# Experts' gate sums: PSUM banks copied by ScalarE and their diagonal picked by transfers, in place of a masked sum on VectorE

## The chip, the cores and the metric

The kernel runs on one NeuronCore of a Trainium2 chip. The metric is the device time of one execution in microseconds; a time is a median over runs. The engines are TensorE (matmuls), VectorE (DVE in the profile), ScalarE (ACT), GpSimd (POOL) and SyncE (SP, here a queue that issues transfers). ScalarE and SP also issue transfers (ACTq and SPq in the profile). Each engine works through its own instructions in the order in which the program wrote them, and a wait holds up everything behind it on that engine.

## The reference

The kernel mixes two branches with a gate. The input x has 2048 tokens of 640 values.

```python
g = sigmoid((x * gate_w).sum(-1, keepdims=True))
a = einsum("ts,se->te", seq_re, x @ hid_re.T) - einsum("ts,se->te", seq_im, x @ hid_im.T)
s1, s2 = scores of 32 heads against two sets of 16 keys (q = x @ w_q, split in two)
top 2 of s1, top 2 of s2 -> 4 sums -> top 2 pairs (e1, e2) -> softmax of the two
b[n] = sum over heads and the two pairs of gate * gelu(x[n] @ u[e]) * v[e],  e = 16 * e1 + e2
out = g * a + (1 - g) * b
```

The kernel doesn't gather rows of u and v. It computes gelu(x u) for all 256 experts, and for each token a table of 256 numbers: the sum of the gates of all (head, pair) choices that fell on expert e. The table multiplies the activations, and a matmul with v gives b. The change concerns only how this table gets from the matmuls that make it into DRAM.

## The kernel before, in words

**The stages.** The Fourier branch is done first along the sequence: two matrices (real, imaginary; `w`), four columns of 512 tokens each (`c`), 16 pieces of 128 source tokens each (`s`), so 128 pieces (`seq_piece`, L200). A piece is 128 x 512 f32 values, loaded by SP five pieces ahead (L158) and split three pieces ahead into a high and a low part: ScalarE writes the high part (L122), GpSimd subtracts (L123). Four buffers `WS` hold split pieces. Five groups of three matmuls (`mm3`, L127 to L129) add the piece into PSUM banks 0 to 4. After 16 pieces ScalarE evicts the five banks to `ST` (L217), VectorE multiplies them by the gate row (`gate_piece`, L191), and ScalarE's queue stores them to `pd` in DRAM (L198). In between the pieces the scores (L409 to L421), the activations (`u_pair`, L528) and the choice of experts (`topk`, `gates`, `rows`) are worked off. The last part, from piece 128 on, multiplies by the hidden matrices in two halves `b` of 35 steps (`step`, L846), with loads of `pd` and sums of them on VectorE (`add_a`, L738), and adds the experts' part (`z_group`, L832).

**The pump.** What VectorE has to do beside the main row is written as generators that yield an estimate of their time. `run_bg` is called after each group of three matmuls with 0.68 (us of TensorE), and adds `share` times this to a credit; as long as the credit is positive the next step is written into the program. The share is 1.25 while the experts run, 0.95 from eight pieces before the last part (`ending`, L935), 0 in the first ten steps of the last part and 1.05 after. Gate pieces, table sums (`make_sums`, L673) and the like take their estimate from the credit. `bg.drain` writes all steps left until a condition holds: at four pieces before the last part, until two of the sets are free (L946), and in `load_z`, until the half's sums are complete (L763).

**The experts.** `experts` (L555) works through 32 sets: two halves `g` of 1024 tokens, 16 chunks `c` of 64 tokens (eight of each of the half's eight 128-token tiles). `build` writes two one-hot f16 tables for a set with three VectorE instructions (L570 to L572): P[r, (e1, t)], which carries the gate, and Q[r, (e2, t)]; rows r are the (part of the gate, choice, head) combinations, 128 of them, and t counts four tokens that are handled together. `use` (L587) multiplies them: 16 matmuls of 128 x 64 by 64 (L594) fill one PSUM bank of 128 partitions x 8 x 64. A partition is (half s, e1, t) and a column (m, e2, t'); only t = t' is wanted, the rest are products of different tokens. Sets are handed out in pairs, singly once `ending` is set. The matmuls of a pair are written after the next pair's tables. Banks 5 and 6 are used in turn (`ps_s`), bank 7 in the last part.

**The sums.** `sums` (L574) takes the diagonal t = t' on VectorE. A mask `mask4` of 128 x 4, with 1/32768 where t' is the partition's t and 0 elsewhere, multiplies the bank (L578, into `tmp`), and a reduction over t' (L580) writes 16 x 8 values per partition into `cd`, a buffer of 128 x 16 x 128. The step is charged 1.4. After the sixteenth chunk of a half SP writes `cd` to `gd` in DRAM with two transfers (L584), one for each 64 partitions. `load_z` (L760) later reads `gd` back, 128 expert rows x 128 tokens at a time (L770), together with the activations and the gate row, on SP's queue.

Of the kernel before, what the change touches and what calls it, by code (L numbers as in the profile page):

```python
# [8 lines left out]
F32 = mybir.dt.float32  # L9
F32R = mybir.dt.float32r  # L10
F16 = mybir.dt.float16
AF = mybir.ActivationFunctionType
OP = mybir.AluOpType
AX = mybir.AxisListType
PSUM = bass.MemoryType.PSUM

P = 128
# [3 lines left out]
E = 16  # L21
# [12 lines left out]
GSCALE = 32768.0  # L34
# [56 lines left out]
def gated_mix_kernel(ctx: ExitStack, tc: tile.TileContext, xT, xn, dreT, dimT, wsre, wsim, wq, kT, uT, vv, gw, out):  # L91
    nc = tc.nc
    ctx.enter_context(tc.manual_schedule())

    const = ctx.enter_context(tc.tile_pool(name="const", bufs=1))
    big = ctx.enter_context(tc.tile_pool(name="big", bufs=1))
    dram = ctx.enter_context(tc.tile_pool(name="dram", bufs=1, space=bass.MemoryType.DRAM))
# [8 lines left out]
    def bank(n, shape=(P, TC), dt=F32):  # L106
        return psum.tile(list(shape), dt, name=f"b{n}", tag=f"b{n}")

    def ps_s(shape=(P, TC)):
        return bank(5 + rotate("pss", 2), shape)  # L110

    def ps_t(shape, dt=F32):
        return bank(7, shape, dt)
# [16 lines left out]

    pd = {(w, c): dram.tile([KD, P, TC], F32, name=f"pd{w}{c}", tag=f"pd{w}{c}") for w in range(2) for c in range(NC)}
    actd = dram.tile([2, P, S], F32, name="actd")
    gd = dram.tile([2, 2, 4, E, E, P], F32, name="gd")
    gdr = dram.tile([S], F32, name="gdr")
    bg = Pump()

# [42 lines left out]
    p3, last_part, ending, share = None, False, False, 0.95  # L179
# [40 lines left out]
    for q in range(2 * NC):  # L220
        n = NT * (q + 1)
# [50 lines left out]
    t = ps_t([P, 512])  # L272
# [12 lines left out]
    for r in range(2):  # L285
# [3 lines left out]
    identf = const.tile([P, P], F32)  # L289
# [3 lines left out]
    wtab4 = const.tile([P, E, 4], F16)  # L293
    nc.gpsimd.iota(wtab4, pattern=[[-1, E], [0, 4]], base=E, channel_multiplier=0,
                   allow_small_or_imprecise_dtypes=True)
    mask4 = const.tile([P, 4], F32)
    nc.vector.tensor_reduce(mask4, identf.rearrange("p (a b) -> p b a", b=4), op=OP.add, axis=AX.X)
    nc.vector.tensor_scalar(mask4, mask4, 1.0 / GSCALE, None, op0=OP.mult)


    wqs, wps, wp = {}, {}, {}
# [68 lines left out]
    n = bursts[-1]  # L370
# [170 lines left out]
    for p in range(NP):  # L541
        n = N0 + 5 * p
# [12 lines left out]
    def experts():  # L555


        shp = [P, 16, E, 4]
        wt = wtab4[:, None].to_broadcast(shp)
        todo = deque((g, c) for g in range(2) for c in range(16))  # L560
        cd = {}

        def build(g, c, s):
            pt, qt = (HOT[s // 2][:, s % 2, n].rearrange("p (m e t) -> p m e t", e=E, t=4) for n in range(2))

            def row(n):
                r = ROWS[g][:, n, 8 * c:8 * c + 8, :].rearrange("p b (s t) -> p (b s) t", t=4)
                return r[:, :, None, :].to_broadcast(shp)

            nc.vector.tensor_tensor(pt, row(0), wt, op=OP.is_equal)  # L570
            nc.vector.tensor_tensor(qt, row(1), wt, op=OP.is_equal)
            nc.vector.tensor_tensor(pt, pt, row(2), op=OP.mult)  # L572

        def sums(g, c, t):  # L574
            if c == 0:
                cd[g] = p3.tile([P, E, P], F32, name="cd", tag="cd")
            tmp = p3.tile([P, 8 * E, 4], F32, name="tmp")
            nc.vector.tensor_tensor(tmp, t.rearrange("p m (e t) -> p (m e) t", t=4),  # L578
                                    mask4[:, None, :].to_broadcast([P, 8 * E, 4]), op=OP.mult)
            nc.vector.tensor_reduce(cd[g][:, :, 8 * c:8 * c + 8].rearrange("p e m -> p m e"),  # L580
                                    tmp.rearrange("p (m e) t -> p m e t", e=E), op=OP.add, axis=AX.X)
            if c == 15:
                for s in range(2):
                    nc.sync.dma_start(gd[g, s].rearrange("t e f m -> e t f m"), cd[g][64 * s:64 * s + 64])  # L584
                summed.add(g)

        def use(group):  # L587
            ts = []
            for g, c, s in group:
                t = bank(7, (P, 8, E * 4)) if last_part else ps_s((P, 8, E * 4))  # L590
                pt, qt = (HOT[s // 2][:, s % 2, n].rearrange("p (m c) -> p m c", m=16) for n in range(2))
                for m in range(16):
                    r = slice(64 * (m % 2), 64 * (m % 2) + 64)
                    nc.tensor.matmul(t[r, m // 2, :], pt[:, m], qt[:, m], start=True, stop=True)  # L594
                ts.append(t)
                free_sets.append(s)
            for (g, c, s), t in zip(group, ts):
                sums(g, c, t)
                yield 1.4

        prev = []
        while todo or prev:
            group = []
            if todo:
                def few():
                    return len([s for s in free_sets if s < 2 or not ending]) < min(len(todo), 1 if ending else 2)
                if few():
                    yield from use(prev)
                    prev = []
                for n in range(min(len(todo), 1 if ending else 2)):  # L610
                    s = min(free_sets) if ending else free_sets[0]
                    free_sets.remove(s)
                    g, c = todo.popleft()
                    group.append((g, c, s))
                    build(g, c, s)
                    yield 3.3
            if prev:
                yield from use(prev)
            prev = group
# [101 lines left out]
    def take(key):  # L721
        if raw_tags:
            t, n = raw_tags.pop(0)
            if t == "wf":
                raw_free.append(big.tile([P, TC], F32, name="ra", tag=t, bufs=5))
            else:
                r = big.tile([P, 2, TC], F32, name="ra", tag=t)
                raw_free.extend(r[:, a] for a in range(2))
        raw[key] = f = raw_free.popleft()
        return f  # L730
# [29 lines left out]
    def load_z(b, n):  # L760

        c = 2 * b + n
        bg.drain(lambda: b in summed)  # L763
        nc.sync.dma_start(take((b, "g", n)), gdr[c * TC:(c + 1) * TC].partition_broadcast(P))
        for k in range(2):
            a, f = take((b, "za", k)), take((b, "zf", k))
            nc.sync.dma_start(a, actd[k][:, c * TC:(c + 1) * TC])
            for i in range(4):
                i8 = (4 * c + i) % 8
                nc.sync.dma_start(f[:, i * P:(i + 1) * P],  # L770
                                  gd[b, i8 // 4, i8 % 4].rearrange("e f m -> (e f) m")[k * P:(k + 1) * P])

    def split_z(b, n):

# [139 lines left out]
    for b in range(2):  # L914
        M = NPC + b * NSTEP
        for k in range(KD):
            at(M - (8 if b else 6) + k, load_a, b, "a11", k, 1, 1)
            at(M - 4 + min(k, 4 if b else 3), load_a, b, "a12", k, 1, 2)
            at(M + k, load_a, b, "s", k, 2, 2)
            at(M + k, load_a, b, "s3", k, 2, 1)  # L920
            at(M + 4 + k, add_a, b, "s", "s3", k, False)
            at(M + 5 + k, load_a, b, "a11", k, 1, 1)
            at(M + 8 + k, add_a, b, "s", "a11", k, False)
            at(M + 8 + k, add_a, b, "s3", "a11", k, True)
            at(M + 8 + k, load_a, b, "a12", k, 1, 2)
            at(M + 13 + k, add_a, b, "s", "a12", k, True)
            at(M + 21 + k, load_a, b, "a22", k, 2, 2)
        for n, i in ((0, -1 if b else 0), (1, 21)):
            at(M + i, load_z, b, n)
            at(M + i + 4, split_z, b, n)  # L930
# [3 lines left out]
    for n in range(N0, NPC):  # L934
# [4 lines left out]
        if n >= N1 and p3 is None and len(rowed) == NT and n % NT not in (NT - 2, NT - 1):  # L939
            p2_stack.close()  # L940
            p3 = ctx.enter_context(tc.tile_pool(name="p3", bufs=1, reuse_waits="tile"))
# [63 lines left out]
```

## Time and profile before

Three runs: median 790.2 us, from 789.94 to 791.78. One execution was profiled:

| | us |
|---|---|
| median of the runs | 790.2 |
| profiled execution: span from the first to the last instruction (no other time of it is shown) | 788.2 |
| TensorE busy (98% of the span) | 773.4 |
| VectorE busy (69%) | 547.3 |
| GpSimd busy (43%) | 341.1 |
| ScalarE busy (35%) | 275.5 |
| experts' matmuls L594, 512 | 11.9 |
| table building L570, L571, L572, 32 each | 28.4, 30.8, 37.3 |
| mask multiply L578 and sum L580, 32 each | 21.9, 22.0 |

Busy time of matmuls is that of pipelined instructions, whose ends are modelled; starts are the surer measure. The mean granted TensorE clock was 0.996 of full speed. The experts' first matmuls start at 479.1 us and their last at 700.9 us. In a row that groups instructions, the form is: line, engine, operation, what is written <- what is read, partitions x elements, count | busy us, mean ns | idle time before, and what ended it.

### The profile page before, as it was taken

What the parts mean: (1) busy time and instruction counts of PE and PEld (TensorE: products, weight loads), DVE (VectorE), ACT (ScalarE), POOL (GpSimd) and SP (SyncE); (2) the same over time, 40 slices, a digit from 0 to 9 for tenths busy, and PEclk for the clock granted to TensorE, in tenths of its full rate; (3) what the DMA queues carried; (4) which work ended last, traced back from release to release, by engine and by line L of the source; (5) the groups of instructions that cost most, each with busy time, mean ns of one, the idle gap of its engine ahead of it and who ended that gap; (6) DMA issues with size and microseconds to landing.
All of it is one profiled execution on the core that took longest, in us unless ns stands there. A gap on an engine that the chain in (4) does not pass through costs nothing.

```text
span 788.2 us, 10943 instructions
## 1 busy us (share of the span) xinstructions
PE 773.4 (98%) x4116; PEld 624.1 (79%) x4116; DVE 547.3 (69%) x660; ACT 275.5 (35%) x445; POOL 341.1 (43%) x233
## 2 busy tenths in 40 slices
PE   8999999999999999999999999999999899999997
PEld 6777677888888888888888888887887787877786
DVE  5741022286887799599979566999999897544851
ACT  5343323321314533342443551311333534513450
POOL 5522324315334242442416774343365484735370
PEclk9999999999999999999999999999999899999999
DMA  9966985502022330315124652322633794439621
GB/s 338 366 253 191 332 322 185 174 13 101 20 96 91 124 114 14 104 61 172 56 83 132 187 168 82 123 91 84 224 125 111 238 301 135 161 82 313 228 85 67
DMA packets 70468, 121.14 MB, mean 154 GB/s; under 512 B 16528, under 2 KB 23568, under 8 KB 70160
## 3 DMA queue, kind: packets, MB, share of 16 engines
q1 hardware_dynamic: 57664, 103.00, 39.8%
q10 hardware_dynamic: 12752, 17.45, 6.3%
q8 instruction: 32, 0.52, 0.3%
q14 instruction: 20, 0.16, 0.1%
HBM read 98.91 MB, written 19.93 MB: 151 GB/s over the span
## 4 chain that ended last, share of the span: by engine, by line
PE 79%; DVE 7%; DMA 5%; issue 3%; POOL 2%; SPq 1%; ACT 1%; ACTq 0%; DVEq 0%; POOLq 0%
PE b L127 26%; PE b L128 25%; PE b L129 25%; PE b L317 2%; DMA ra<-pd 2%; DVE hot L572 1%; POOL WS L123 1%; DMA out_y<-ST 1%; DVE ST L191 1%; DVE ra L739 1%; DVE hot L570 1%; DVE cd L580 1%; PE b L594 1%; DMA gd<-cd 1%; DMA wf<-in_wsre 1%
## 5 line engine op out<-in xcount | busy, mean ns | idle before, releaser
L123 POOL TENSOR_TENSOR WS<-wf,WS 128x512 fp32r<-128x512 f32 x127 | 188.9, 1493 | 275.6 <-ACT WS L122 260.0
L127 PE MATMUL b<-WS,X 128*128 128x512 f32 x635 | 252.2, 397 | 0.1
L128 PE MATMUL b<-WS,X 128*128 128x512 f32 x635 | 248.7, 392 | 0.4 <-POOL WS L123 0.4
L129 PE MATMUL b<-WS,X 128*128 128x512 f32 x635 | 248.4, 391 | 0.0
L127 PEld LDWEIGHTS b<-WS,X 128*128 128x128 f32 x635 | 119.8, 189 | 33.3 <-issue 7.8
L129 PEld LDWEIGHTS b<-WS,X 128*128 128x128 f32 x635 | 119.8, 189 | 25.6
L128 PEld LDWEIGHTS b<-WS,X 128*128 128x128 f32 x635 | 119.9, 189 | 24.9 <-POOL WS L123 1.3
L122 ACT ACTIVATE WS<-wf 128x512 fp32r<-128x512 f32 x128 | 80.2, 629 | 124.0 <-PE b L129 71.6
L434 DVE TENSOR_REDUCE mm<-sc 128x64 f32<-128x1024 f32 x32 | 39.0, 1218 | 45.6 <-ACT sc L420 45.1
L123 POOL TENSOR_TENSOR xl<-xf,xh 128x640 fp32r<-128x640 f32 x16 | 33.0, 2086 | 70.0 <-ACT xh L122 63.4
L123 POOL TENSOR_TENSOR WS<-ra,WS 128x512 fp32r<-128x512 f32 x32 | 48.7, 1544 | 31.5 <-ACT WS L122 28.2
L129 PE MATMUL b<-WU,xl 128*128 128x512 f32 x160 | 62.3, 389 | 0.0
L128 PE MATMUL b<-WU,xh 128*128 128x512 f32 x160 | 62.3, 389 | 0.0
L127 PE MATMUL b<-WU,xh 128*128 128x512 f32 x160 | 62.2, 389 | 0.0
L420 ACT ACTIVATE sc<-b 128x512 f32<-128x512 f32 x32 | 20.8, 649 | 101.8 <-PE b L129 94.8
L191 DVE SCALAR_TENSOR_TENSOR ST<-ST,grow 128x512 f32<-128x512 f32 x40 | 37.0, 989 | 16.9 <-DMA grow<-gdr 16.9
L332 DVE TENSOR_TENSOR WU<-b,WU 128x512 fp32r<-128x512 f32 (+1 forms) x16 | 7.8, 490 | 56.7 <-ACT WU L331 56.7
L436 DVE TENSOR_TENSOR eq<-sc,mm 128x1024 f16<-128x1024 f32 x32 | 45.3, 1416 | 1.1
L123 POOL TENSOR_TENSOR WP<-ra,WP 128x512 fp32r<-128x512 f32 x18 | 29.0, 1617 | 27.8 <-ACT WP L122 27.8
L500 ACT ACTIVATE rows<-rt 128x384 f16<-128x384 f16 x16 | 31.0, 1970 | 25.9 <-DMA rt<-gs 25.9
L122 ACT ACTIVATE WS<-ra 128x512 fp32r<-128x512 f32 x46 | 28.1, 629 | 33.5 <-DVE ra L739 9.3
L440 DVE TENSOR_REDUCE rr<-eq 128x64 f16<-128x1024 f16 x32 | 39.0, 1220 | 1.1
(144 smaller groups left out, 1232.0 us busy)
## 6 DMA issues: line engine op xcount, KB each, us to landing
wq<-in_wq SPq DMA_DIRECT2D x32, 640.0 KB, 6.5
ra<-pd SPq DMA_DIRECT2D x70, 256.0 KB, 4.7
wf<-in_wsre SPq DMA_DIRECT2D x64, 256.0 KB, 5.3
wf<-in_wsim SPq DMA_DIRECT2D x64, 256.0 KB, 3.4
pd<-ST ACTq DMA_DIRECT2D x40, 256.0 KB, 3.1
xr<-in_xn SPq DMA_DIRECT2D x16, 320.0 KB, 6.0
xf<-in_xT SPq DMA_DIRECT2D x16, 320.0 KB, 3.1
out_y<-ST ACTq DMA_DIRECT2D x7, 512.0 KB, 3.4
```

The source lines that it names most:

```text
L122: nc.scalar.activation(h, f, AF.Copy)
L123: eng.tensor_sub(l, f, h.bitcast(F32))
L127: nc.tensor.matmul(o, wh, ah, start=first, stop=False, skip_group_check=more)
L128: nc.tensor.matmul(o, wh, al, start=False, stop=False, skip_group_check=more)
L129: nc.tensor.matmul(o, wl, ah, start=False, stop=last, skip_group_check=more)
L191: nc.vector.scalar_tensor_tensor(f, f, -1.0 if w else 1.0, g, op0=OP.mult, op1=OP.mult)
L317: nc.tensor.matmul(ps[32 * j:32 * j + 32, :HALF], kp[:, 8 * G // H, r, :], w[:, j], start=(r == 0), stop=(r == 1))
L420: nc.scalar.activation(scs[i].rearrange("p h e -> p (h e)")[:, c], ps, AF.Copy)
L434: nc.vector.tensor_reduce(m, sc, op=OP.max, axis=AX.X)
L436: nc.vector.tensor_tensor(eq, sc, m[:, :, None].to_broadcast([P, HH, E]), op=OP.is_equal)
L440: nc.vector.tensor_reduce(r, eq, op=OP.max, axis=AX.X)
L500: nc.scalar.activation(ROWS[i // 8][:, :, :, i % 8], t, AF.Copy)
```

## The change

- `mask4` and its two instructions at the start go.
- In `sums`, ScalarE copies the whole bank (all 512 columns of 128 partitions, scaled by 1/32768) to SBUF, with the columns reordered from (m, e2, t') to (e2, t', m). `cd` now holds four chunks, 128 x 16 x 4 x 32, and a new one is taken for every four chunks; the pool keeps one buffer, as before.
- After every fourth chunk ScalarE's queue issues four transfers, one for each t: they take partitions t, t+4, t+8, ... and of these the columns with t' = t. That is the diagonal. One transfer is 32 partitions x 16 x 32 values, rows of 128 bytes. Before, it was rows of 512 bytes.
- `gd` has its second and third axes swapped, and `load_z` reads it accordingly.
- The step is charged 0.2 in place of 1.4 to the pump's credit.

```diff
-    gd = dram.tile([2, 2, 4, E, E, P], F32, name="gd")
+    gd = dram.tile([2, 4, 2, E, E, P], F32, name="gd")
...
-    mask4 = const.tile([P, 4], F32)
-    nc.vector.tensor_reduce(mask4, identf.rearrange("p (a b) -> p b a", b=4), op=OP.add, axis=AX.X)
-    nc.vector.tensor_scalar(mask4, mask4, 1.0 / GSCALE, None, op0=OP.mult)
...
         def sums(g, c, t):
-            if c == 0:
-                cd[g] = p3.tile([P, E, P], F32, name="cd", tag="cd")
-            tmp = p3.tile([P, 8 * E, 4], F32, name="tmp")
-            nc.vector.tensor_tensor(tmp, t.rearrange("p m (e t) -> p (m e) t", t=4),
-                                    mask4[:, None, :].to_broadcast([P, 8 * E, 4]), op=OP.mult)
-            nc.vector.tensor_reduce(cd[g][:, :, 8 * c:8 * c + 8].rearrange("p e m -> p m e"),
-                                    tmp.rearrange("p (m e) t -> p m e t", e=E), op=OP.add, axis=AX.X)
+            if c % 4 == 0:
+                cd[g] = p3.tile([P, E, 4, 4 * 8], F32, name="cd", tag="cd")
+            o = cd[g][:, :, :, 8 * (c % 4):8 * (c % 4) + 8]
+            nc.scalar.activation(o.rearrange("p f t m -> p (f t) m"), t.rearrange("p m c -> p c m"), AF.Copy,
+                                 scale=1.0 / GSCALE)
+            if c % 4 == 3:
+                w = slice(32 * (c // 4), 32 * (c // 4) + 32)
+                for n in range(4):
+                    nc.scalar.dma_start(gd[g, n, :, :, :, w].rearrange("s e f m -> (s e) f m"), cd[g][n::4, :, n, :])
             if c == 15:
-                for s in range(2):
-                    nc.sync.dma_start(gd[g, s].rearrange("t e f m -> e t f m"), cd[g][64 * s:64 * s + 64])
                 summed.add(g)
...
                 sums(g, c, t)
-                yield 1.4
+                yield 0.2
...
                 nc.sync.dma_start(f[:, i * P:(i + 1) * P],
-                                  gd[b, i8 // 4, i8 % 4].rearrange("e f m -> (e f) m")[k * P:(k + 1) * P])
+                                  gd[b, i8 % 4, i8 // 4].rearrange("e f m -> (e f) m")[k * P:(k + 1) * P])
```

## The prediction

> **What bounds the kernel now.** First the page's busy times, then PE's own waits (columns: who waited, for what, total us, times, longest us).
>
> ```profile
> PE 773.4 (98%) x4116; PEld 624.1 (79%) x4116; DVE 547.3 (69%) x660; ACT 275.5 (35%) x445; POOL 341.1 (43%) x233
> ```
>
> ```profile
> PE b L594 <- DVE tmp L578: 4.1, 1, 4.1
> PE b L127 <- ACT ST L891: 3.0, 2, 1.6
> ```
>
> TensorE is the bound; only what takes a hole out of its row, or puts one in, changes the time. The holes are few. The largest is a wait of the experts' matmuls for VectorE's mask multiply, the instruction that the change deletes. TensorE's order in time (start us, duration us, instruction, count, and in brackets the idle time before it):
>
> ```profile
> 479.07 0.70 PE L594 MATMUL b<-hot 128*64 128x64 f16 x32
> 487.41 0.69 PE L594 MATMUL b<-hot 128*64 128x64 f16 x32
> ...
> 557.47 0.69 PE L594 MATMUL b<-hot 128*64 128x64 f16 x32
> 568.53 0.70 PE L594 MATMUL b<-hot 128*64 128x64 f16 x32
> ...
> 613.08 0.64 PE L594 MATMUL b<-hot 128*64 128x64 f16 x16 [4.15 <-DVE tmp L578]
> 613.64 0.80 PE L127 MATMUL b<-WS,X 128*128 128x512 f32 x1
> ...
> 618.85 0.39 PE L127 MATMUL b<-WS,X 128*128 128x512 f32 x1
> ...
> 624.79 0.39 PE L129 MATMUL b<-WS,X 128*128 128x512 f32 x1
> ...
> 626.98 0.39 PE L127 MATMUL b<-WP,DD 128*128 128x512 f32 x1
> ```
>
> The hole costs more than its 4.15 us. From 618.85 to 624.79 there are 26 steps, 0.228 us each: the normal pace, so 3.4 us for a sequence piece of 15. The 12 matmuls from 613.64 to 618.85 took 5.21 us, where 12 x 0.228 = 2.74 would do: **2.5 us lost to a lower clock after the hole**. The stage rows agree (columns: stretch, its length, then busy us and count of PE, PEld, DVE, ACT and POOL, granted clock, DMA share, GB/s):
>
> ```profile
> 500.00:550.00 50.00, 50.00 (x392) 40.23 (x391) 48.66 (x62) 9.92 (x17) 19.62 (x14) 1.00 0.31 96
> 550.00:600.00 50.00, 50.00 (x306) 40.78 (x306) 48.46 (x68) 16.21 (x33) 22.92 (x18) 1.00 0.48 162
> ```
>
> ```profile
> 610.00:620.00 10.00, 6.92 (x33) 5.56 (x33) 9.79 (x16) 4.43 (x9) 5.65 (x5) 0.66 0.60 187
> ```
>
> ```profile
> 640.00:650.00 10.00, 10.00 (x46) 8.29 (x45) 9.97 (x7) 4.02 (x8) 10.00 (x7) 1.00 0.93 317
> ```
>
> The granted clock is 0.66 at the hole and 1.00 before it. VectorE was busy 97.1 of the 100 us ahead of it: it built expert sets and summed them slightly slower than the pump handed them out, fell behind, and the forced drain four pieces before the last part found it late.
>
> **The change, part by part.** Columns of these groups: busy us, mean ns | idle before.
>
> ```profile
> L578 DVE TENSOR_TENSOR tmp<-b,mask 128x512 f32<-128x512 f32 x32 | 21.9, 685 | 25.3 <-PE b L594 24.1
> L580 DVE TENSOR_REDUCE cd<-tmp 128x128 f32<-128x512 f32 x32 | 22.0, 689 | 1.9 <-DMA gd<-cd 0.7
> L217 ACT ACTIVATE ST<-b 128x512 f32<-128x512 f32 x40 | 22.9, 599 | 3.5 <-PE b L129 1.7
> L122 ACT ACTIVATE WS<-wf 128x512 fp32r<-128x512 f32 x128 | 80.2, 629 | 124.0 <-PE b L129 71.6 <-issue 16.1 <-DMA wf<-in_wsre 10.0
> L123 POOL TENSOR_TENSOR WS<-wf,WS 128x512 fp32r<-128x512 f32 x127 | 188.9, 1493 | 275.6 <-ACT WS L122 260.0 <-DMA rt<-gs 8.1 <-DVE dp L469 2.6
> L500 ACT ACTIVATE rows<-rt 128x384 f16<-128x384 f16 x16 | 31.0, 1970 | 25.9 <-DMA rt<-gs 25.9
> ```
>
> *VectorE.* 32 x (0.685 + 0.689) = 44.0 us leave it. Hidden under TensorE, worth only the hole it made. The mask's two small instructions at the start go too; no hole hangs on them, zero.
>
> *The pump.* The charge per set falls from 3.3 + 1.4 to 3.3 + 0.2, at 1.25 us of charge per us of TensorE. A pair now takes 9.4/1.25 = 7.52 us plus its own matmuls; the rows show 8.34 (479.07 to 487.41), so these cost 0.82. After: 7.0/1.25 + 0.82 = 6.42 us. From 479.07, the sixteenth and last pair is used at 479.07 + 15 x 6.42 = 575.4, plus what two gate pieces add (557.47 to 568.53 is 2.7 more than 8.34; 5.4 for both), plus one table-sum step of the last columns (4.0 charged, 3.2 us): **about 584**. The last part starts at 626.98 now; eight pieces of 3.4 us and the hole's 6.65 earlier, and a few sets' matmuls, is 591, and from there sets are handed out singly. So all sums are issued before that point and the drain finds nothing. Per pair VectorE then has 8.34 less 4 x 0.69 = at most 5.6 us of building in 6.42 us, so it should not fall behind. The hole and its slow clock go: **-6.65 us**. That the sets after 600 come in pairs and not singly saves TensorE some bubbles, under 1 us at 0.82 a pair; I leave it out.
>
> *ScalarE's copies.* The trace has no copy that reads PSUM in steps of 64 elements and writes runs of 8. Bounds: 0.60 us (L217, same size, contiguous) and, by L500's 1.97/384 = 5.1 ns an element, 2.6 us. L500 writes single f16 values 16 bytes apart; the new copy writes eight f32 in a row, nearer to L217. I take 0.65: 1.3 us in each 6.42, where ScalarE has 26.1 us of other work per 100. Off the path.
>
> [...]
>
> *The spills.* Issues and landings (issues: ns min/median/max and first and last start; second fence: KB each, median us to landing):
>
> ```profile
> L198 ACTq DMA_DIRECT2D pd<-ST x40: 326/327/834, 109.4 to 636.2; - x40
> ```
>
> ```profile
> gd<-cd SPq DMA_DIRECT2D x4, 512.0 KB, 5.1
> gdr<-gt ACTq DMA_DIRECT2D x1, 8.0 KB, 12.3
> ```
>
> Four transfers of 512 KB (1,024 rows of 512 B) on SP become 32 of 64 KB (512 rows of 128 B) on ScalarE's queue: 8 groups of four, 2,048 rows per group. Issuing: 4 x 0.33 to 0.83 = 1.3 to 3.3 us of ScalarE per group, I take 1.6. Landing: two old transfers back to back are also 2,048 rows and landed in 5.1 us in the middle; the gate's 2,048 rows of one value took 12.3. So 5 to 12 us, I take 8. The 12,288 rows more run in a stretch where the engines are busy 0.31 to 0.48 of the time; the pieces' loads run two pieces ahead of their splits, 6.8 us, and I give this no price of its own.
>
> One buffer is kept, so the first copy of a group of four waits until the previous spill has been read. It comes 6.42 us after the pair whose copies (1.3 us after matmuls of 0.7) and issues (1.6) precede the landing: the block is 0.7 + 1.3 + 1.6 + 8 - (6.42 + 0.7) = 4.5 us, with bounds 1.2 and 10.2. **What is queued behind it:** the f32 splits of the sequence pieces, three pieces ahead: 3 x 3.4 = 10.2 us less 0.63 on ScalarE (L122) and 1.5 on POOL (L123) leave 8 us. Hidden, except at the end of a column, where five evictions must follow TensorE: a bank is rewritten four steps of 0.68 after its end, less 0.66, so only 2 us of cover. There are two such ends in the stretch:
>
> ```profile
> 498.74 3.32 ACT L217 ACTIVATE ST<-b 128x512 f32<-128x512 f32 x5
> ```
>
> ```profile
> 559.10 3.33 ACT L217 ACTIVATE ST<-b 128x512 f32<-128x512 f32 x5 [0.84 <-PE b L129]
> ```
>
> By my times pair four (a spill) falls at 498.3 and pair thirteen (a waiting copy) at 479.07 + 12 x 6.42 + 2.7 = 558.8. One of them catching 2 to 4 us is as likely as not: I charge **+1.7 us**.
>
> [...]
>
> *SP's queue.* Removing its spills also frees loads behind them (first fence: who waited for what, total us, times, longest; then SP's and TensorE's order in time):
>
> ```profile
> SPq L584 <- DVE cd L580: 40.6, 2, 26.5
> ```
>
> ```profile
> 702.56 2.96 SPq L584 DMA_DIRECT2D gd<-cd  x2
> 705.61 4.01 SPq L736 DMA_DIRECT2D ra<-pd  x3
> ```
>
> ```profile
> 654.32 0.50 PE L127 MATMUL b<-WS,DD 128*128 128x512 f32 x1 [1.34 <-ACT ST L891]
> ...
> 725.83 0.49 PE L128 MATMUL b<-WS,DD 128*128 128x512 f32 x1 [1.37 <-POOL WS L123]
> 735.01 0.50 PE L127 MATMUL b<-WS,DD 128*128 128x512 f32 x1 [1.62 <-ACT ST L891]
> ```
>
> SP stood 26.5 us until 702.56 for the last sums, and the loads of the second half came after it; the hole at 725.83 follows, and should go: **-1.4**. The two behind ScalarE's L891 (1.34, 1.62) hang on VectorE's adds and on loads in a stretch with DMA at 0.93 and POOL full. VectorE enters it without backlog; I count half: **-1.5**.
>
> **Sum.** -6.65 - 1.4 - 1.5 + 1.7 = -7.85 on a span of 788.2, so 780.3. The three runs have a median of 790.2, 2.0 above the span; the profiled run has no other time shown. Forecast **782 us**.
>
> **Rivals.**
> 1. *The gain is handed back* (0.14). The last part starts 6.6 us sooner and loads at a DMA share of 0.93 and POOL at 10.00 of 10 hold it up; two or three holes of 1.5 us appear. About 786.
> 2. *No change* (0.09): a pump that finishes late. If ScalarE's block keeps banks 5 and 6 full, TensorE waits for it, four or so times 2 us: 790.
> 3. *ScalarE becomes the bound* (0.16), the slower end. At 2.6 us a copy, a pair asks 5.2 + 0.8 (issues) + 1.7 (26.1% of 6.42) = 7.7 us of ScalarE in 6.42: over 16 pairs 20 us late, less 8 of cover, plus blocks of at least 1.2 us at seven groups, 8 more: 20 us, less the 9.55 gained (6.65 + 1.4 + 1.5): 801. It begins at a copy of (6.42 - 2.5)/2 = 2.0 us and outweighs the gain from about 2.3. For it: L500's row. Against it: L217's, of the same size and type. The same end is reached by long spills: the block is 3.5 us shorter than the spill, so it passes the cover of 8 at 11.5, and at seven groups eats the gain from about 13.
> 4. *The change doesn't move the drain* (counted in 2): if pairs go at 7 us or more, singles remain at 591 and the hole shrinks only.
>
> **How the numbers follow.** Forecast 0.61, rivals 0.14, 0.09, 0.16. What a measurement can tell from no change is 0.3%, 2.4 us: 787.8 to 792.6. Forecast and rival 1 are faster, less a little: 0.73; rival 2 makes 0.10; rival 3 makes 0.17. The floor is every hole and the slow clock gone, 790.2 - 6.65 - 4.33 - 1 = 778. The range runs from there to 790, over rivals 1 and 2; the forecast's own is 778 to 785.
>
> **What would show it.** Right: no 4.15 us hole near 609 and a clock of 1.00 there; pairs 6.4 us apart; sixteen of x32 and none of x16; L578 and L580 gone; new copies at 0.6 to 0.7 us; SP waiting nowhere for sums. Wrong: copies above 2 us, splits late (TensorE waiting for ScalarE's or POOL's WS between 485 and 590), or spills landing later than 11.5 us after issue.

## The result, and the profile after

The changed kernel takes **778.0 us** (four runs, 777.57 to 778.43) against 790.1 us before: a ratio of 0.985, with a 95% interval of 0.9833 to 0.9867. It is faster by about 12 us. The profiled execution took 778.1 us, with a span of 776.3, so 1.8 us lie around the span.

Line numbers of the changed kernel are three lower from the mask's place on: the experts' matmuls L594 are now L591, the copies are L575, the spills L580, L891 is L888.

The page's busy times after:

```profile
PE 769.5 (99%) x4116; PEld 622.0 (80%) x4116; DVE 500.5 (64%) x594; ACT 291.9 (38%) x477; POOL 341.0 (44%) x233
```

TensorE's one wait of more than 0.1 us after the first 17 us (who waited, for what, total us, times, longest us):

```profile
PE b L127 <- ACT ST L217: 0.7, 1, 0.7
```

The wait for VectorE's multiply is gone, and so are the waits behind L891. TensorE's order in time:

```profile
479.41 0.70 PE L591 MATMUL b<-hot 128*64 128x64 f16 x32
485.70 0.69 PE L591 MATMUL b<-hot 128*64 128x64 f16 x32
...
503.95 0.50 PE L127 MATMUL b<-WS,X 128*128 128x512 f32 x1 [0.66 <-ACT ST L217]
...
580.21 0.69 PE L591 MATMUL b<-hot 128*64 128x64 f16 x32
```

Pairs come 6.29 us apart, the last at 580.2; after it TensorE has no hole up to its last matmuls. The stages that held the holes before (stretch, length, busy us and count of PE, PEld, DVE, ACT, POOL, granted clock, DMA share, GB/s):

```profile
600.00:630.00 30.00, 30.00 (x134) 24.84 (x133) 21.68 (x26) 14.69 (x29) 20.77 (x16) 1.00 0.76 248
...
715.00:740.00 25.00, 25.00 (x112) 20.67 (x112) 14.63 (x23) 9.07 (x16) 9.43 (x6) 1.00 0.40 127
```

**Where the 11.9 us of span went.** The hole at the drain and its slow clock: 6.65. The last part's holes: 1.34, 0.22, 1.37 and 1.62, together 4.55. One new hole: -0.66. That is 10.5. The remaining 1.4 can be found by laying the starts of TensorE's main row in the two traces side by side. Three pairs of sets (0.83 us each) stand where six single sets stood (0.59 us each, 1.1 for the two at the drain): about 1.0. The first steps after a hole are slower, by 0.27 us in all, and one hole stands where four stood: 0.8. The experts' first matmuls start 0.3 us later: -0.3.

What took VectorE's place. First the operations on `cd`: ns min/median/max, first and last start, then who its engines waited for and the landing of the spills:

```profile
L575 ACT ACTIVATE cd<-b x32: 590/596/605, 480.0 to 581.2; 128x512 f32<-128x512 f32 x32
L580 ACTq DMA_DIRECT2D gd<-cd x32: 517/647/1192, 487.3 to 583.8; - x32
its engine sat idle before it (us, times) until:
  PE b L591: 21.1, 15
...
DMA to landing us min/median/max: 2.0/2.5/3.9
```

A copy takes 0.596 us, what a contiguous eviction takes (0.60 for L217). Before its copies ScalarE waited for TensorE and never for a spill: the one buffer holds nothing up. What costs is the issuing. ScalarE's order in time around the new hole (start, us, instruction, count, idle before):

```profile
499.07 0.60 ACT L217 ACTIVATE ST<-b 128x512 f32<-128x512 f32 x1
499.57 1.08 ACT L575 ACTIVATE cd<-b 128x512 f32<-128x512 f32 x2
500.68 2.58 ACTq L580 DMA_DIRECT2D gd<-cd  x4
503.30 2.07 ACT L217 ACTIVATE ST<-b 128x512 f32<-128x512 f32 x4 [2.65 <-PE b L129]
```

A column ends here. One bank is evicted, then two copies (1.08) and four issues (2.58) stand ahead of the other four evictions. They are 3.7 us late. TensorE came for the second bank at 503.29 (503.95 less the hole). Without the delay, an eviction that follows the first at once would have freed it at about 500.2. So 3.1 us were covered, more than the 2 us of the prediction, because this pair's matmuls (498.97, 0.70 us) stand between the two columns. The rest is the hole of 0.66.

### The profile page after: what moved, and what is told of

Same layout as the page of the kernel before. It is cut to its first block, busy times and chain, and to the rows that moved or that the text cites. A ratio compares the mean times of both kernels' runs of the same rounds, so it can differ in the third digit from the quotient of the medians.

```text
span 776.3 us, 10941 instructions
## 1 busy us (share of the span) xinstructions
PE 769.5 (99%) x4116; PEld 622.0 (80%) x4116; DVE 500.5 (64%) x594; ACT 291.9 (38%) x477; POOL 341.0 (44%) x233
## 4 chain that ended last, share of the span: by engine, by line
PE 96%; ACT 1%; POOL 1%; DMA 1%; SPq 0%; ACTq 0%; issue 0%; DVE 0%; DVEq 0%; POOLq 0%
PE b L127 31%; PE b L128 30%; PE b L129 30%; PE b L314 3%; PE b L591 1%; DMA wf<-in_wsre 1%; PE b L326 1%; POOL WS L123 0%; ACTq L580 0%; ACT ST L217 0%; POOL kp L286 0%; ACT L384 0%; ACT WS L122 0%; SPq L235 0%; ACT cd L575 0%
## 5 line engine op out<-in xcount | busy, mean ns | idle before, releaser
L417 ACT ACTIVATE sc<-b 128x512 f32<-128x512 f32 x32 | 20.8, 650 | 101.9 <-PE b L129 100.6
L123 POOL TENSOR_TENSOR WS<-ra,WS 128x512 fp32r<-128x512 f32 x32 | 46.3, 1469 | 27.1 <-ACT WS L122 26.7
L567 DVE TENSOR_TENSOR hot<-rows,wtab 128x1024 f16<-128x1024 f16 x32 | 32.0, 1001 | 38.6 <-PE b L591 38.6
L736 DVE TENSOR_TENSOR ra<-ra 128x512 f32<-128x512 f32 x40 | 38.4, 1006 | 10.6 <-POOL WS L123 7.4
L191 DVE SCALAR_TENSOR_TENSOR ST<-ST,grow 128x512 f32<-128x512 f32 x40 | 32.0, 854 | 18.3 <-DMA grow<-gdr 11.6
```

The costliest lines, as they stand in the source:

```text
L123: eng.tensor_sub(l, f, h.bitcast(F32))
L191: nc.vector.scalar_tensor_tensor(f, f, -1.0 if w else 1.0, g, op0=OP.mult, op1=OP.mult)
L417: nc.scalar.activation(scs[i].rearrange("p h e -> p (h e)")[:, c], ps, AF.Copy)
L736: nc.vector.tensor_add(raw[b, o, k], raw[b, o, k], raw[b, what, k])
```

## The experiments

Each kernel was timed beside the kernel before on the same chip. All of them compute the full result. In the first four runs that kernel had a median of 789.9 us, in the last four 790.0.

**1. The charge alone.** The kernel before, VectorE's sums kept, pairs asked for as fast as in the changed one.

```diff
                 sums(g, c, t)
-                yield 1.4
+                yield 0.2
```

> The kernel before with one number changed: a set's sums are charged 0.2 to the pump in place of 1.4; VectorE still does the masked sums, SP still spills. Theory (VectorE's load is the cause): pairs are now asked for every 6.4 us, but VectorE needs 5.6 us of tables and 2.75 us of sums for each, 8.4 us. Its lead of 13 us is used up after six or seven pairs, and from there TensorE waits about 2 us per pair, 15 to 20 us in all with a lower clock between: 795 to 810 us. Rival (the pump's charge alone brings the gain, because all sets are out of the way before sets are handed out singly): no hole at the drain, 779 to 783 us.

Measured: **795.2 us** (793.66 to 795.46), ratio 1.0063 (1.0039 to 1.0087): slower than before. TensorE's waits, and its steps after the last of them in order of time:

```profile
PE b L594 <- DVE tmp L578: 10.0, 8, 2.4
```

```profile
594.30 0.80 PE L127 MATMUL b<-WS,X 128*128 128x512 f32 x1
...
599.13 0.39 PE L129 MATMUL b<-WS,X 128*128 128x512 f32 x1
```

Eight holes, 10.0 us where 15 to 20 were expected, all for the mask multiply; the 11 matmuls from 594.30 to 599.13 took 4.83 us where 2.51 is normal. The theory holds, with the time at the lower edge of its range: VectorE cannot serve pairs every 6.3 us while it also sums them. The rival is out: the charge by itself makes the kernel slower. One thing speaks for the early finish: with all sets done by 594 the last part had no hole, although VectorE did its 44 us.

**2. The copies with the old charge.** The changed kernel, pairs as far apart as before.

```diff
                 sums(g, c, t)
-                yield 0.2
+                yield 1.4
```

> The changed kernel with the charge put back to 1.4: ScalarE copies and spills, VectorE is relieved, but pairs come 8.3 us apart and the last sets are handed out singly as late as about 690 us. Theory (VectorE's load is the cause): the hole at the drain is gone, since VectorE has only 5.6 us of work per 8.3 us; 6.65 us less than before at the least, and the holes of the last part go as far as they came from VectorE's backlog and from SP waiting for sums: 778 to 783 us. Rival (the charge): the drain still finds six sets left and TensorE waits there, now for ScalarE: 786 to 790 us.

Measured: **780.2 us** (779.15 to 781.17), ratio 0.9877 (0.9849 to 0.9906).

```profile
PE b L127 <- ACT ST L217: 1.0, 1, 1.0
PE b L127 <- ACT ST L888: 0.5, 1, 0.5
```

```profile
479.22 0.69 PE L591 MATMUL b<-hot 128*64 128x64 f16 x32
487.55 0.69 PE L591 MATMUL b<-hot 128*64 128x64 f16 x32
...
694.59 0.44 PE L591 MATMUL b<-hot 128*64 128x64 f16 x16
```

Pairs are 8.33 us apart again and the last set comes at 694.6, yet the drain makes no hole. So **the copies together with their spills on ScalarE's queue are worth about 10 us, and the charge about 2 on top**. Of the 2, holes make 0.9 (1.04 and 0.52 here, 0.66 there); four single sets here in place of two pairs, and the slower steps after one hole more, make the rest, by the costs above. This run moves the spills off SP's queue as well, so its 10 us are not VectorE's relief alone: run 3 tells the two apart. The charge and the copies are not independent: the charge costs 5 us without the copies and gains 2 with them.

**3. The spills alone.** The kernel before, its four transfers issued by ScalarE.

```diff
-                    nc.sync.dma_start(gd[g, s].rearrange("t e f m -> e t f m"), cd[g][64 * s:64 * s + 64])
+                    nc.scalar.dma_start(gd[g, s].rearrange("t e f m -> e t f m"), cd[g][64 * s:64 * s + 64])
```

> The kernel before with only its four spills moved from SP's queue to ScalarE's. Theory (SP's wait of 26.5 us for the last sums made the loads of the second half late): the holes at 724 and 726 us (0.22 and 1.37) go and perhaps the one at 735 (1.62), the hole at the drain stays: 787 to 789 us. Rival (those holes come from VectorE's adds or from full DMA engines): 790 us, or more where ScalarE now waits for VectorE's last sums.

Measured: **785.5 us** (784.90 to 787.12, seven runs), ratio 0.9949 (0.9934 to 0.9963), 1.5 us below the expected range. TensorE's holes, in order of time:

```profile
613.63 0.64 PE L594 MATMUL b<-hot 128*64 128x64 f16 x16 [3.64 <-DVE tmp L578]
...
654.60 0.50 PE L127 MATMUL b<-WS,DD 128*128 128x512 f32 x1 [1.35 <-ACT ST L891]
...
707.64 0.50 PE L127 MATMUL b<-WS,DD 128*128 128x512 f32 x1 [0.63 <-ACT ST L891]
```

The drain's hole stays, and so does the one at 654. The three of the second half (0.22, 1.37, 1.62) are gone, with one of 0.63 in their place. So the second half's holes came from SP's queue, all three of them, and the drain's hole did not: it takes the copies to remove that one. The profiled run took 787.1 with a span of 785.3, 2.9 below the span of before. The holes make 3.1 of that (3.21 less 0.63, and 0.51 at the drain) and the slower steps after them some 0.8; a wait of 1.0 us for a weight load (`wq`, read by L317, whose matmuls are over by 129 us in the kernel before), long before any spill, takes 1.0 back. The median is lower than this by another 1.5 us, and that goes with the clock: five of the seven executions had a mean granted clock of 0.998 and took 784.9 to 786.1, two had 0.996 and took 787.0 and 787.1. At equal clock the gain over the kernel before is 3.1 us (785.4 against 788.5 at 0.998, 787.1 against 790.1 at 0.996). SP still stood for the table itself, 24.5 us until 707.4. That did no harm: all thirteen loads of `pd` ahead of this wait went out without a break from 669, where before three of the thirteen stood behind the spill.

```profile
669.06 8.72 SPq L736 DMA_DIRECT2D ra<-pd  x13
```

The hole near 654 has another chain. Here it ends in the same wait for L891 as in the kernel before, of which these are ScalarE's rows:

```profile
653.15 0.63 ACT L122 ACTIVATE WS<-ra 128x512 fp32r<-128x512 f32 x1 [4.46 <-DVE ra L739]
653.69 0.58 ACT L891 ACTIVATE ST<-b 128x512 f32<-128x512 f32 x1
```

The eviction that TensorE waits for stands behind a split, and the split waits for an add on VectorE. The hole is 1.35 here, 0.52 with the copies at the old charge, and absent in run 1, where VectorE's sums were over early, and in the changed kernel. So VectorE's backlog makes it in these kernels. It is not the only thing that can: in run 5 it is back with 1.91 us, and there VectorE was busy 21.54 of the 30 us from 630 on, near the changed kernel's 20.37 and not the 27.59 of before.

**4. The changed kernel with its spills on SP's queue.**

```diff
-                    nc.scalar.dma_start(gd[g, n, :, :, :, w].rearrange("s e f m -> (s e) f m"), cd[g][n::4, :, n, :])
+                    nc.sync.dma_start(gd[g, n, :, :, :, w].rearrange("s e f m -> (s e) f m"), cd[g][n::4, :, n, :])
```

> The changed kernel with its 32 spills on SP's queue in place of ScalarE's. Theory (the hole of 0.66 us at the end of a column comes from four issues, 2.6 us, that stand ahead of the evictions on ScalarE): that hole goes, 777.0 to 777.8 us. Rival (SP, which runs ahead, now waits for copies and sends the pieces' loads late): TensorE waits for splits at some of the eight spills, 779 to 784 us.

Measured: **776.9 us** (776.45 to 777.60), ratio 0.9836 (0.9813 to 0.9859), 0.1 us under the expected range. The end of the column on ScalarE is now

```profile
499.90 1.08 ACT L575 ACTIVATE cd<-b 128x512 f32<-128x512 f32 x2
500.93 2.65 ACT L217 ACTIVATE ST<-b 128x512 f32<-128x512 f32 x4
```

and TensorE's wait for L217 is gone. It was timed again beside the changed kernel, on one chip, five rounds:

> The changed kernel again, as the partner of the next run on the same chip: 777.5 to 778.5 us.

> The changed kernel with its spills on SP's queue, again, beside the changed kernel itself: the hole of 0.66 us at the end of a column is gone in each profile, so 0.5 to 1.1 us less than the changed kernel. Rival (the 1.1 us seen between separate runs is chance): no difference beyond 0.3 us.

Measured: **778.9 us** for the changed kernel (777.26 to 779.70) and **777.6 us** with the spills on SP (776.02 to 778.51); ratios to before 0.9851 (0.983 to 0.9873) and 0.9839 (0.9817 to 0.986). The first lies 0.4 us above its expected range. The medians differ by 1.1 and 1.3 us in the two comparisons, the expected way (the second 0.2 more than expected), but the intervals overlap. The hole of 0.66 is gone in both profiles; that the time follows is likely, not shown. A wait for a weight load (`wq`), which neither edit touches, was absent in one of these four profiles and 0.7 to 1.5 us in the others, and scatters the times.

**5. A dearer copy, 1.8 and 3.0 us a set.** How far is ScalarE from being the bound? Every copy was repeated, three times and five times.

```diff
-            nc.scalar.activation(o.rearrange("p f t m -> p (f t) m"), t.rearrange("p m c -> p c m"), AF.Copy,
-                                 scale=1.0 / GSCALE)
+            for _ in range(3):
+                nc.scalar.activation(o.rearrange("p f t m -> p (f t) m"), t.rearrange("p m c -> p c m"), AF.Copy,
+                                     scale=1.0 / GSCALE)
```

> The changed kernel with every copy of a bank made three times over (the same data to the same place), so ScalarE spends about 1.65 us on a set in place of 0.55. Theory (ScalarE is covered by the splits' lead of 8 us, but by only 2 us at the end of a column): a pair asks 3.3 us of copies, 1.3 of issues and 1.7 of other work in 6.3 us, just full; between column ends TensorE stays without holes, and at the two ends in the stretch the copies and issues ahead of the evictions make holes of 1 to 4 us: 780 to 785 us. Rival (ScalarE has no influence at this load): 778 us.

Measured: **789.7 us** (785.89 to 791.09, ten runs), ratio 0.9991 (0.9973 to 1.0009): the whole gain gone, 5 us above the expected range. TensorE's holes, and ScalarE at the first of them (this kernel's lines are one higher from the copy on):

```profile
508.24 0.79 PE L127 MATMUL b<-WS,X 128*128 128x512 f32 x1 [4.17 <-ACT ST L217]
...
573.26 0.50 PE L127 MATMUL b<-WS,X 128*128 128x512 f32 x1 [1.77 <-ACT ST L217]
...
658.81 0.50 PE L127 MATMUL b<-WS,DD 128*128 128x512 f32 x1 [1.91 <-ACT ST L889]
```

```profile
501.34 3.60 ACT L576 ACTIVATE cd<-b 128x512 f32<-128x512 f32 x6
504.97 2.57 ACTq L581 DMA_DIRECT2D gd<-cd  x4
```

The two holes at column ends came as expected (4.17 and 1.77), and between them TensorE ran on. What the expectation lacked: a lower clock after the hole of 4.17, and a hole of 1.91 in the last part. The profile shows one slow stretch there, 8 matmuls from 508.24 to 511.70 us, 3.46 us where 1.82 is normal (mean clock 0.998 over the span); other executions had a mean clock down to 0.994 and took up to 791.1.

> The changed kernel with every copy made five times over, about 2.7 us of ScalarE per set, which is the price of the slower rival in the prediction (2.6 us). Theory (that rival's mechanism holds, only its price was wrong): a pair asks 5.5 us of copies, 1.3 of issues and 1.7 of other work, 8.5 us in 6.3: some 35 us too much over 16 pairs, less 8 of cover, and a lower clock after holes: 797 to 810 us, slower than before. Rival (TensorE's wait for copies only shifts the pairs, and the main row's slack takes it up): below 790 us.

Measured: **826.9 us** (824.90 to 828.92), ratio 1.0465 (1.0431 to 1.0499), above the expected range.

```profile
PE b L592 <- ACT cd L576: 20.8, 8, 4.9
PE b L127 <- ACT ST L217: 10.9, 2, 5.8
```

```profile
500.00:550.00 50.00, 36.37 (x280) 28.47 (x279) 26.05 (x34) 37.27 (x66) 12.64 (x9) 0.89 0.30 84
```

The slower rival's mechanism is real, but two thirds of its holes are not where the prediction had them. It let TensorE wait for late splits, which have 8 us of cover. TensorE waited for **banks**: the next pair's matmuls need the two banks that ScalarE has not yet copied (20.8 us), which is how the prediction's rival 2 had it. And the granted clock was 0.89 on average from 500 to 550 us, which no term of the prediction had.

## Why the prediction was right, and where a size was off

The direction, the mechanism and the range held; the forecast of 782 was 4 us above the result, which lies on the floor of 778 that the prediction gave.

- **The drain's hole and its slow clock, -6.65.** Gone, as worked out. Run 2 has no hole there at the old charge, and run 3, with the spills moved but the sums still on VectorE, keeps 3.64 us of it: VectorE's relief does it. Run 1 shows that the charge alone does the opposite. The prediction did not separate the two; it argued from VectorE's load and priced the pump by its charge, and both were needed for its account of the pairs.
- **The pump, 6.42 us a pair, the last near 584.** 6.29 and 580.2.
- **VectorE, 44.0 us.** Its busy time fell by 46.8, and it now waits 38.6 us for sets to come free.
- **The copies, 0.65 us.** 0.596. The upper bound, taken from a copy that writes single f16 values 16 bytes apart, was no measure for this one. The reads in steps of 256 bytes cost nothing that shows: the contiguous L217 takes 0.599.
- **The spills, +1.7.** Mis-sized, and for another reason than given. Taken were 1.6 us of issuing and 8 us of landing for a group of four, 9.6 together. Measured were 2.6 of issuing, and a whole group had landed 4.1 to 5.0 us after its first issue. The wait on the one buffer, which carried most of the charge, did not occur. The 0.66 us that did come are due to the issuing, at the column end that the prediction named (pair four, 498.3; it came at 499.0). The gate's 12.3 us for 2,048 rows of one value was no measure for rows of 128 bytes: one transfer of 64 KB in such rows landed in 2.5 us, where a read of `gd`, 64 KB in rows of 512, takes 2.4.
- **SP's queue, -1.4 for the hole at 725.83.** Right, and too small: run 3 shows that the holes of 0.22 and 1.62 hang on it too. The spills are now over by 584, and the reads of the second half's table are issued 35 us sooner (711.74 before):

```profile
676.82 2.28 SPq L767 DMA_DIRECT2D ra<-gd  x4
...
679.65 2.75 SPq L767 DMA_DIRECT2D ra<-gd  x4
```

- **The two holes behind L891, -1.5, half of them.** Both went, -2.96: one with VectorE's backlog, one with SP's wait. The step that failed is the halving "in a stretch with DMA at 0.93 and POOL full". The last part starts 4.5 us sooner and nothing was handed back (rival 1). The full stretch is still there, 7 us sooner, with the DMA engines and GpSimd about as busy as before (a DMA share of 0.96 and 9.68 us of 10, where it was 0.93 and 10.00). What differs is VectorE: 4.20 us busy of 10, where it was 9.97. So full DMA engines and a full GpSimd alone made no hole here:

```profile
633.00:643.00 10.00, 10.00 (x46) 8.28 (x45) 4.20 (x3) 5.49 (x11) 9.68 (x8) 1.00 0.96 339
```

- **Left out as under 1 us:** the bubbles of single sets. They are about 1.0 of the 1.4 us that lie outside the holes, three pairs in place of six single sets.

In sum: 1.7 us too little for the last part, 1.0 too much for ScalarE, 1.4 left out. That is the 4 us; all three errors lean the same way.

**The slower rival** was rightly kept: it begins earlier than the prediction said. It put the point where the gain is lost at 2.3 us a copy; at 1.8 us a set the gain is gone (run 5).

## What to carry to other kernels

When TensorE is 98% busy, list its holes one by one with what ended each: here their sum with the slow clock after them, 11.2 us, was nearly all that this change beside TensorE's own work won (11.9 us of span). It removed all the holes of the experts and of the last part, and put in one of 0.66. Relieve the busy engine first and hand its work out sooner only then: the charge that gained 2 us with the relief cost 5 without it, while the copies and their spills gained 10 at the old charge. And when work is moved to an engine that also frees PSUM banks and evicts accumulators, price its latency at those two places and count the issues of transfers as work: here 2.6 us for four issues mattered, the landing of rows of 128 bytes, 2.5 us a transfer, did not.

## What the runs showed of the hardware that was not expected

**The size of a hole alone did not decide whether the clock fell.** Lone holes of 1.34 to 1.91 us left the granted clock at 1.00 in the stages around them (before, and run 5). But in run 1 two holes of 1.75 and 1.08 us, with 0.4 us of matmuls between, were followed by a lower one, and so was a lone hole of 1.67 us:

```profile
530.64 0.54 PE L594 MATMUL b<-hot 128*64 128x64 f16 x16 [1.08 <-DVE tmp L578]
531.11 0.80 PE L127 MATMUL b<-WS,X 128*128 128x512 f32 x1
...
534.25 0.40 PE L128 MATMUL b<-WS,X 128*128 128x512 f32 x1
...
547.31 0.44 PE L594 MATMUL b<-hot 128*64 128x64 f16 x16 [1.67 <-DVE tmp L578]
547.68 0.64 PE L127 MATMUL b<-WS,X 128*128 128x512 f32 x1
...
551.43 0.40 PE L127 MATMUL b<-WS,X 128*128 128x512 f32 x1
```

The steps in between are 0.427 us in place of 0.228, and the mean granted clock is 0.66 from 530 to 535 us and 0.79 and 0.87 in the two stages of 5 us from 545 on. What decides beside the size was not shown. By the starts of its matmuls, a fall of the clock cost 1.5 us (run 1, the 7 matmuls from 531.11 to 534.25) to 2.5 us (the drain of the kernel before).

**ScalarE's copies, which read PSUM in steps of 256 bytes, were as fast as its contiguous evictions**: 596 ns for 512 columns against 599 ns (L217). **Rows of 128 bytes from SBUF to DRAM** landed about as fast as the reads of `gd`, the other transfers of 64 KB (2.5 against 2.4 us). The issue on ScalarE was dearer, 0.65 us for 512 rows against 0.33 for the stores of `pd`. The number of rows alone does not explain it: SP issued the spills of the kernel before, 1,024 rows each, in 0.61 us in the middle (L584), and those of run 4, 512 rows each, in 0.62.
